# A fused attention and two-layer MLP kernel: block products of the second layer in pairs on two banks, its side work spread, the weights' sums read later

## The chip, the core and the metric

The kernel runs on one core of a Trainium2 chip. The metric is device time in microseconds (us) of one execution; the figure before is the median of three runs. Engines are named as in the profile: PE (TensorE's matmuls), PEld (TensorE's weight loads), DVE (VectorE), ACT (ScalarE), SPq (the queue of SyncE, which issues the DMAs here).

## What is computed

Eight batches of eight heads read 32 states by attention and are read by them; the result, 4352 tokens of 512 features, goes through two MLPs with squared ReLU. All of it is float32, and matmuls run as three products of split operands (a high part in fp32r and the rest), so that each product of the reference is three matmuls.

```python
def _attn_ref(x, state):                    # (8, 8, 512, 64), (8, 8, 32, 64)
    scores = scale * np.matmul(x, state.transpose(0, 1, 3, 2))
    ...softmax...;  xread = np.matmul(a, state)
    scores2 = scale * np.matmul(state, x.transpose(0, 1, 3, 2))
    ...softmax...;  sread = np.matmul(a2, x)
    return np.concatenate([xread, sread], axis=2)

x = attn_out.transpose(0, 2, 1, 3).reshape(B * S, H * D)
h = np.maximum(x @ w_in, 0.0);  x = (s * (h * h) + b) @ w_out     # first MLP: 512 -> 2048 -> 512
h = np.maximum(x @ w_in2, 0.0); out = h * h @ w_out2              # second MLP
```

## The kernel before

**The first layer** goes in steps (j, f): batch j (0 to 7, and 8 for the states' tokens) and one of 16 blocks f of 128 hidden features. A step is `mm1(j, f)` (six matmuls of 512 columns into a bank, twelve of 256 columns for j = 8), `relu2` on ACT (Relu out of the bank, Square, and Copy to the high part g), `low` on DVE (the rest of g), and `mm2` of the step two before (`LAG` = 2): twelve matmuls into four banks. I call the sixteen steps of one j a head. Work beside is hung on steps by `at_step(step, fn, rank)` and runs after the step's matmuls, in the order of rank. In heads 1 to 6 that is the attention of batch j + 1 (`att_sc` at step 3, `att_exp` and `att_norm` at 5 and 7, `att_turn` at 9 and 11, S products with two banks each at 5, 9, 13), and reading 16 pieces each of the second layer's weights `i2` and `o2` (`load_2`: a load one step, its conversion in a buffer `v` the next, and a DMA back to memory). From `i2` the sums that the block products need are made for each of eight pairs u of blocks: `sums_load` reads, `sums_add` makes four sums on DVE (tile `wt`), and seven `sums_out` each take a tile `wset`, write its high part on ACT and the rest on DVE, and send it to `w2s`. `v`, `wset` and, from step (6, 4) on, a running sum `wsum` share the pool `vp` of three buffers. Banks of `mm1`, S, scores and transposes come in turn from a cycle of four.

**The second layer** goes over six parts of up to six token tiles (the last has four) and over eight units in each, 48 in all. A unit makes two blocks of hidden features from two halves of the tokens by seven block products in the place of eight (`PRODUCTS` = 1, 6, 2, 5, 7, 3, 4). `product` is six matmuls of 384 columns (256 in the last part). Products 1, 2, 7 and 4 go to the bank A, of pool `psa`; 6, 5 and 3 to B, of `psb`; 2 adds onto 1, 3 onto 5 and 4 onto 7 in place, once what was there has been read. So one unit runs A B A B A B A, and the next begins with A. After each product ACT or DVE reads the bank, and DVE squares with max(c, 0) * c; `put_g` splits the square into the high part on ACT and the rest on DVE. The four quarters of a unit (L679, L690, L694, L697) are in the tiles `g`, which the second product `mm2_second` of the next unit reads: 36 matmuls of 512 columns (24 in the last part), of which five or six stand behind each of the seven products. Between units of a part nothing else is due; in unit 5 the next part's x is loaded, in unit 6 it gets its bias (`x_bias`) and eight differences (`x_sums`, at two products), and in unit 7 each product is followed by `x_split` of the same number: two high parts on ACT, two rests on DVE, 28 in all. For the first part all this and `o2`'s first three quarters (`load_w2`) are done in head 8, the last quarter in unit 0.

Everything is in the order of the program (`manual_schedule`): each engine takes its instructions in the order written, and waits at the head of its queue.

Of the kernel before, what the change touches and what calls it, by code (L numbers as in the profile page):

```python
# [47 lines left out]
LAG = 2  # L48
# [13 lines left out]
def attn_mlp2(ctx: ExitStack, tc: tile.TileContext, xT, xn, st, w_in1, w_out1, w_in2, w_out2, s_in, b_in, out):  # L62
# [390 lines left out]
    def mm2(j, f, g):  # L453
# [7 lines left out]
        for t in range(KD):  # L461
            sl = slice(t * P, (t + 1) * P)
            ops = [(wh[:, sl], g[:, 0]), (wh[:, sl], g[:, 1]), (wl[:, sl], g[:, 0])]
            o = acc_t[0][t][:, :n]
            for i, (l_, r_) in enumerate(ops):
                nc.tensor.matmul(out=o, lhsT=l_, rhs=r_, start=(opens and i == 0), stop=(closes and i == 2))  # L466
            if closes:
                evac(j, t, o, j < 2 and f >= CUTS[1])
# [99 lines left out]
    def x_sums(n, i, t1, t2, t3):  # L568
# [3 lines left out]
        nc.vector.tensor_tensor(out=t1, in0=a[:, th:], in1=a[:, :th], op=ALU.subtract)  # L572
        nc.vector.tensor_tensor(out=t3, in0=b[:, th:], in1=a[:, th:], op=ALU.subtract)
        nc.vector.tensor_tensor(out=t2, in0=b[:, th:], in1=t1, op=ALU.subtract)
        nc.vector.tensor_tensor(out=a[:, th:], in0=b[:, :th], in1=t2, op=ALU.subtract)
        X["t", i] = {1: a[:, :th], 2: b[:, :th], 3: b[:, th:], 4: a[:, th:], 5: t1, 6: t2, 7: t3}

    def x_split(n, m):
        v = x_view(n, m)
        for i in range(2):  # L580
            split(v[:, 0, i], v[:, 1, i], X["t", i][PRODUCTS[m]])
# [24 lines left out]
    def put_g(i, f, k, c):  # L606

        th = half(units[i][0])
        slot = xw["g", (2 * i + f) % 3]
        if k == 0:  # L610
            g2[i, f] = slot[:, : 4 * th].rearrange("p (h t) -> p h t", h=2)
        v = g2[i, f][:, :, k * th : (k + 1) * th]
        split(v[:, 0], v[:, 1], c)
# [39 lines left out]
    def second_layer(between):  # L653

        for i, (n, u) in enumerate(units):
            th = half(n)
            nn = n + 1 if n + 1 < len(parts) else None
            before = mm2_second(i - 1) if i else iter(())
            count = 6 * len(parts[units[i - 1][0]]) if i else 0
            done = 0  # L660
            c = {}
            for m, p in enumerate(PRODUCTS):
                if p == 1:
                    c["A"] = pst("A", psa)[:, :th]
                elif p == 6 or p == 5:
                    c["B"] = pst("B", psb)[:, :th]
                elif p == 7:
                    c["A"] = pst("A", psa)[:, :th]
                product(i, m, c["A" if p in (1, 2, 7, 4) else "B"], p in (1, 6, 5, 7))
                if p == 1:  # L670
                    c["m1"] = c_tile(vp, "v", th)
                    nc.scalar.copy(out=c["m1"], in_=c["A"])
                elif p == 6:
                    c["u2"] = c_tile(rp, "r", th)
                    nc.vector.tensor_tensor(out=c["u2"], in0=c["B"], in1=c["m1"], op=ALU.add)  # L675
                elif p == 2:
                    r = c_tile(at, "sc", th)
                    nc.scalar.activation(out=r, in_=c["A"], func=ACTF.Relu)
                    nc.vector.scalar_tensor_tensor(out=r, in0=c["A"], scalar=0.0, in1=r, op0=ALU.max, op1=ALU.mult)  # L679
                    c["11"] = r  # L680
                elif p == 5:
                    c["m5"] = c_tile(vp, "v", th)
                    nc.scalar.copy(out=c["m5"], in_=c["B"])
                    put_g(i, 0, 0, c["11"])
                elif p == 7:
                    c["u3"] = c_tile(vp, "v", th)
                    nc.vector.tensor_tensor(out=c["u3"], in0=c["A"], in1=c["u2"], op=ALU.add)
                elif p == 3:
                    r = c_tile(at, "sc", th)
# [293 lines left out]
```

## Time and profile before

| what | us |
|---|---|
| median of three runs (1463.84 to 1467.78) | 1465.83 |
| the profiled execution, whole | 1467.13 |
| its span, first to last instruction | 1465.3 |
| mean granted TensorE clock, share of full | 0.981 |
| PE busy | 1402.2 (96%) |
| PEld, DVE, ACT busy | 1165.5, 854.5, 641.8 |

PE is busy for almost the whole span, so the time is read from what PE does: how far apart its matmuls start, where it waits, for whom, and at which granted clock. In the timeline each row is a run of like instructions with its start, its length and, in brackets, the idle time of its engine ahead of it and what ended it. A matmul's end is modelled: a matmul of 512 columns shows as 0.39 us, and the next starts 0.23 us after it. So an idle time in brackets is some 0.16 us shorter than what the wait really took from PE.

### The profile page before, as it was taken

To read this page: it belongs to the slowest core of one execution; us is meant where nothing else is said; L and a number is where in the kernel's file an instruction comes from. 1 tells how busy PE (TensorE), PEld (TensorE's weight loads), DVE (VectorE), ACT (ScalarE), POOL (GpSimd) and SP (SyncE) were. 2 spreads that over 40 slices of the span, in tenths; PEclk is the share of its full clock that TensorE was granted. 3 is DMA by queue.
4 is the path that set the end of the run, shared out by engine and by line. 5 is a ranking of instruction groups with operands and counts; after the bars stand their busy time and mean duration, and the time that the engine had idled before them with its cause. 6 is when DMAs were issued, how large, how long until landed. Compare 5 with 4: busy or idle time off the path is not lost.

```text
span 1465.3 us, 20387 instructions
## 1 busy us (share of the span) xinstructions
PE 1402.2 (96%) x7770; PEld 1165.5 (80%) x7770; DVE 854.5 (58%) x1639; ACT 641.8 (44%) x1252; POOL 0.7 (0%) x7
## 2 busy tenths in 40 slices
PE   4999999999899999999899999999999999999998
PEld 2777777767677776889798888888888888888887
DVE  7887636466565648666534654565465447445544
ACT  4777646466566646557512322232232223222322
POOL 0000000000000000000000000000000000000000
PEclk7899999999999999999899999999999999999999
DMA  7355232535445342323635354534444453543652
GB/s 250 108 198 175 72 112 61 166 113 168 155 141 194 116 170 93 107 81 123 230 101 164 110 161 123 163 118 142 144 119 155 129 160 107 159 136 101 203 148 73
DMA packets 94017, 203.18 MB, mean 139 GB/s; under 512 B 9184, under 2 KB 26592, under 8 KB 90848
## 3 DMA queue, kind: packets, MB, share of 16 engines
q1 hardware_dynamic: 93920, 201.89, 43.2%
q8 instruction: 61, 1.00, 0.3%
q14 instruction: 36, 0.29, 0.1%
HBM read 158.86 MB, written 42.99 MB: 138 GB/s over the span
## 4 chain that ended last, share of the span: by engine, by line
PE 79%; DVE 10%; DMA 5%; ACT 4%; issue 1%; SPq 1%; ACTq 0%; DVEq 0%
PE o L631 22%; PE acc L466 20%; PE A L594 12%; PE h L436 11%; PE B L594 9%; PE S L255 1%; PE sr L401 1%; DMA w2s<-wset 1%; DMA xT<-xT 1%; DVE sc L604 1%; DVE sc L690 1%; DMA o2r<-w_out 1%; DMA i<-v 1%; DMA i2r<-w_in 1%; DMA ws<-i 1%
## 5 line engine op out<-in xcount | busy, mean ns | idle before, releaser
L466 PE MATMUL acc<-g,o1h 128*128 128x512 f32 (+1 forms) x1152 | 345.0, 382 | 1.9 <-ACT g L445 1.3
L466 PEld LDWEIGHTS acc<-g,o1h 128*128 128x128 f32 x1152 | 213.4, 190 | 46.8 <-issue 2.2
L436 PE MATMUL h<-aT,S 128*128 128x512 f32 x768 | 207.2, 406 | 15.0 <-ACT r L443 9.8
L466 PE MATMUL acc<-g,o1l 128*128 128x512 f32 (+1 forms) x576 | 219.0, 380 | 0.4 <-DVE o1l L189 0.4
L436 PEld LDWEIGHTS h<-aT,S 128*128 128x128 f32 x768 | 143.1, 192 | 66.9 <-issue 12.5
L449 DVE TENSOR_TENSOR g<-r,g 128x512 fp32r<-128x512 f32 (+1 forms) x144 | 95.1, 661 | 155.0 <-ACT g L445 152.3
L466 PEld LDWEIGHTS acc<-g,o1l 128*128 128x128 f32 x576 | 109.2, 190 | 21.6 <-DVE o1l L189 0.9
L631 PE MATMUL o<-o2h,xw('g', 0)_6560 128*128 128x512 f32 x364 | 124.5, 395 | 0.0
L631 PE MATMUL o<-o2h,xw('g', 1)_6561 128*128 128x512 f32 x364 | 123.7, 393 | 0.0
L631 PE MATMUL o<-o2h,xw('g', 2)_6562 128*128 128x512 f32 x360 | 122.6, 393 | 0.0
L443 ACT ACTIVATE r<-h 128x512 f32<-128x512 f32 (+1 forms) x144 | 81.8, 568 | 84.3 <-PE h L436 82.0
L594 PE MATMUL A<-xw 128*128 128x384 f32 (+1 forms) x576 | 112.8, 330 | 4.4 <-DVE t L697 3.7
L594 PEld LDWEIGHTS A<-xw 128*128 128x128 f32 x576 | 98.9, 188 | 16.7 <-DVE t L697 9.4
L444 ACT ACTIVATE r<-r 128x512 f32<-128x512 f32 (+1 forms) x144 | 87.6, 608 | 4.6
L445 ACT ACTIVATE g<-r 128x512 fp32r<-128x512 f32 (+1 forms) x144 | 87.6, 608 | 4.6
L594 PE MATMUL B<-xw 128*128 128x384 f32 (+1 forms) x432 | 84.1, 329 | 0.2 <-DVE r L675 0.2
L594 PEld LDWEIGHTS B<-xw 128*128 128x128 f32 x432 | 75.7, 188 | 6.2 <-DVE r L675 0.6
L631 PEld LDWEIGHTS o<-o2h,xw('g', 0)_6560 128*128 128x128 f32 x364 | 68.1, 189 | 9.9
L631 PEld LDWEIGHTS o<-o2h,xw('g', 1)_6561 128*128 128x128 f32 x364 | 67.6, 188 | 10.0
L594 PE MATMUL A<-xw,xw('odd', 0)_6433 128*128 128x384 f32 (+1 forms) x288 | 58.2, 337 | 17.3 <-DVE t L697 17.3
L631 PEld LDWEIGHTS o<-o2h,xw('g', 2)_6562 128*128 128x128 f32 x360 | 66.9, 188 | 9.8
L631 PE MATMUL o<-o2l,xw('g', 0)_6560 128*128 128x512 f32 x182 | 72.1, 396 | 0.0
(147 smaller groups left out, 2013.7 us busy)
## 6 DMA issues: line engine op xcount, KB each, us to landing
xw<-w2s SPq DMA_DIRECT2D x168, 256.0 KB, 2.7
xw('odd', 0)_6433<-w2s SPq DMA_DIRECT2D x24, 1024.0 KB, 5.0
xw('odd', 1)_6434<-w2s SPq DMA_DIRECT2D x24, 768.0 KB, 4.3
w2s<-wset SPq DMA_DIRECT2D x56, 256.0 KB, 2.3
i1r<-w_in SPq DMA_DIRECT2D x16, 512.0 KB, 4.9
xT<-xT SPq DMA_DIRECT2D x16, 512.0 KB, 5.7
xn<-xn SPq DMA_DIRECT2D x8, 1024.0 KB, 8.1
o1r<-w_out SPq DMA_DIRECT2D x16, 512.0 KB, 4.3
```

The costliest lines, as they stand in the source:

```text
L255: nc.tensor.matmul(out=outs[r][k * NS : (k + 1) * NS], lhsT=state[rows, r, k, :], rhs=moving(rows, k), start=True, stop=True, skip_group_c ...
L401: nc.tensor.matmul(out=srp[r * D : (r + 1) * D, k * NS : (k + 1) * NS], lhsT=n[:, i, h * D : (h + 1) * D], rhs=a2Ts[r][:, i, k * NS : (k + ...
L436: nc.tensor.matmul(out=hp, lhsT=l_, rhs=r_, start=(i == 0), stop=(i == len(ops) - 1))
L443: nc.scalar.activation(out=r, in_=hp, func=ACTF.Relu)
L444: nc.scalar.activation(out=r, in_=r, func=ACTF.Square)
L445: nc.scalar.activation(out=g[:, 0], in_=r, func=ACTF.Copy)
L449: nc.vector.tensor_tensor(out=g[:, 1], in0=r, in1=g[:, 0].bitcast(F32), op=ALU.subtract)
L466: nc.tensor.matmul(out=o, lhsT=l_, rhs=r_, start=(opens and i == 0), stop=(closes and i == 2))
L594: nc.tensor.matmul(out=o, lhsT=w[:, a, k, :], rhs=x[:, b, k, :], start=(start and k + a + b == 0), stop=(k + a == 2), skip_group_check=True,)
L604: nc.vector.scalar_tensor_tensor(out=c, in0=c, scalar=0.0, in1=c, op0=ALU.max, op1=ALU.mult)
L631: nc.tensor.matmul(out=acc2[t], lhsT=l_, rhs=r_, start=(fa == 0 and e == 0), stop=(fa == NF - 1 and e == 2))
L690: nc.vector.tensor_tensor(out=r, in0=c["B"], in1=c["u2"], op=ALU.add)
```

## The change

It makes no product less or more. (1) In the second layer the banks alternate with every product, across units too; two products stand in a row (a pair), and behind each pair ten or eleven matmuls of the second product. (2) The last two steps' `mm2` of the first layer (24 matmuls, the generator `rest`) are taken out of its end and stand as shares between the products of unit 0. (3) The drain is written anew: out of bank 1 + 2 DVE no longer multiplies; Relu, and Square on ACT in two instructions, for three quarters of four; the split's two halves stand a product or more behind each other. (4) `x_load` moves from unit 5 to unit 3, `x_bias` from 6 to 4, `x_sums` is dealt out singly over units 5 and 6, and `x_split`'s 28 instructions over eleven products, of which the last four are the next part's first. (5) `o2`'s second to fourth quarter are read and split in units 0 to 2. (6) The sums of pair u are loaded, added and sent at head 3 + u // 2, from step 1 or 9: added four steps after the load, and sent one per step at seven steps, where it was two per step at four.

```diff
+        flow = [(rest, 2 * KD * 3)]
+        def drain(i, m, out):
+            p, th = PRODUCTS[m], half(units[i][0])
+            ...
+            if p == 1:
+                c["m1"] = c_tile(vp, "v", th)
+                act(c["m1"], out, ACTF.Copy)
+            elif p == 6:
+                add(c["u2"], out, c["m1"])
+            elif p == 2:
+                act(r, out, ACTF.Relu)
+                after[i, m + 1] = [lambda: act(r, r, ACTF.Square), lambda: g_hi(i, 0, 0, r)]
+                after[i, m + 2] = [lambda: g_lo(i, 0, 0, r)]
+            ...
+            elif p == 3:
+                add(r, out, c["u2"])
+                add(q, c["u3"], c["m5"])
+                act(r, r, ACTF.Relu)
+                act(r, r, ACTF.Square)
+                g_hi(i, 0, 1, r)
+                after[i, m + 1] = [lambda: g_lo(i, 0, 1, r), lambda: square(q)]
+                after[i + 1, 0] = [lambda: g_hi(i, 1, 1, q)]
+                after[i + 1, 1] = [lambda: g_lo(i, 1, 1, q)]
+            elif p == 4:
+                add(r, out, c["u2"])
+                after[i + 1, 0] = [
+                    lambda: act(r, r, ACTF.Relu), lambda: act(r, r, ACTF.Square), lambda: g_hi(i, 1, 0, r)
+                ] + after[i + 1, 0]
...
+            job(3, 6, lambda: x_load(n))
+            for k in range(KD):
+                job(4, 3 + k, lambda k=k: x_bias(k))
+            job(5, 0, begin)
+            for e in range(8):
+                job(5, 1 + 3 * e // 2, lambda e=e: sums[e]())
+            for e in range(count):
+                m, i = e // 2, e % 2
+                job(7, 11 * e // count, lambda m=m, i=i: x_hi(n, m, i))
+                job(7, 11 * e // count + 1, lambda m=m, i=i: x_lo(n, m, i))
...
+                step = i * len(PRODUCTS) + m
+                pool = (psa, psb)[step % 2]
+                if p in (1, 6, 5, 7):
+                    c[p] = pst(f"m{p}", pool)[:, :th]
+                out = c[{2: 1, 3: 5, 4: 7}.get(p, p)]
+                product(i, m, out, p in (1, 6, 5, 7))
+                drain(i, m, out)
+                if step % 2:
+                    while len(flow) > 1:
+                        for _ in flow.pop(0)[0]:
+                            pass
+                        done = 0
+                    upto = flow[0][1] * (m + 1) // len(PRODUCTS)
...
-    for u, (j, f) in enumerate(((2, 13), (3, 5), (3, 12), (4, 3), (4, 10), (5, 1), (5, 9), (6, 1))):
+    for u in range(NF // 2):
+        at0 = step(3 + u // 2, 8 if u % 2 else 0)
         box = {}
-        at_step(step(j, f), lambda u=u, box=box: box.update(raw=sums_load(u)), 7)
-        at_step(step(j, f) + 2, lambda u=u, box=box: box.update(src=sums_add(u, box["raw"])), 8)
+        at_step(at0 + 1, lambda u=u, box=box: box.update(raw=sums_load(u)), 7)
+        at_step(at0 + 5, lambda u=u, box=box: box.update(src=sums_add(u, box["raw"])), 8)
         for m in range(len(PRODUCTS)):
-            at_step(step(j, f) + 3 + m // 2, lambda u=u, m=m, box=box: sums_out(u, m, box["src"]), 8)
+            at_step(at0 + 6 + m, lambda u=u, m=m, box=box: sums_out(u, m, box["src"]), 8)
...
-            if q < 3:
-                at_step(s8 + 11 + 2 * q + h, load, 9)
-                at_step(s8 + 13 + 2 * q + h, cut, 9)
+            if q < 1:
+                at_step(s8 + 11 + h, load, 9)
+                at_step(s8 + 13 + h, cut, 9)
             else:
-                between.setdefault((0, h), []).append(load)
-                between.setdefault((0, 4 + h), []).append(cut)
+                between.setdefault((q - 1, 3 * h), []).append(load)
+                between.setdefault((q - 1, 3 * h + 3), []).append(cut)
```

How the order of three queues moves: on PE, the end of unit 0 and the beginning of unit 1, before (xw is the tile with a product's weights and x, the odd unit's weights are in xw('odd', 0)):

```order
L594 MATMUL A<-xw_6129 128x384 x6
L594 MATMUL B<-xw_6285 128x384 x6
L594 MATMUL A<-xw_6286 128x384 x6
L594 MATMUL A<-xw_5994,xw('odd', 0)_6433 128x384 x6
L631 MATMUL o_6697<-o2h_6468,xw('g', 0)_6560 128x512
L631 MATMUL o_6697<-o2l_6469,xw('g', 0)_6560 128x512
L631 MATMUL o_6697<-o2h_6468,xw('g', 0)_6560 128x512
L631 MATMUL o_6698<-o2h_6468,xw('g', 0)_6560 128x512
L631 MATMUL o_6698<-o2l_6469,xw('g', 0)_6560 128x512
L594 MATMUL B<-xw_5995,xw('odd', 0)_6433 128x384 x6
```

The same place after (the acc rows are `rest`, of the first layer):

```order
L610 MATMUL m_6603<-xw_6129 128x384 x6
L610 MATMUL m_6578<-xw_6285 128x384 x6
L466 MATMUL acc_6028<-g,o1h_1267 128x256
L466 MATMUL acc_6028<-g,o1l_1268 128x256
L466 MATMUL acc_6029<-g,o1h_1267 128x256 x2
L466 MATMUL acc_6029<-g,o1l_1268 128x256
L466 MATMUL acc_6030<-g,o1h_1267 128x256 x2
L610 MATMUL m_6603<-xw_6286 128x384 x6
L610 MATMUL m_6654<-xw_5994,xw('odd', 0)_6433 128x384 x6
```

The product that opens unit 1 (the one that reads `xw('odd', 0)`) wrote the same bank as the one ahead of it, and now writes the other; the seven matmuls of the first layer stand between the pairs.

On DVE, the end of unit 7 of the first part (`xw5` and `xw6` are `x_split`'s rests for the next part, L697 is the read that frees bank A for the next unit's first product), before:

```order
L694 TENSOR_TENSOR t1_7512<-v_7490,v_7470 128x384
L111 TENSOR_TENSOR xw5_6285<-x12_7200,xw5_6285 128x384
L111 TENSOR_TENSOR xw5_6285<-x13_7203,xw5_6285 128x384
L697 TENSOR_TENSOR t1_7530<-A_7483,r_7433 128x384
L604 SCALAR_TENSOR_TENSOR t1_7530<-t1_7530 128x384
L111 TENSOR_TENSOR xw('g', 0)_6560<-t1_7530,xw('g', 0)_6560 128x384
L604 SCALAR_TENSOR_TENSOR t1_7512<-t1_7512 128x384
L111 TENSOR_TENSOR xw('g', 0)_6560<-t1_7512,xw('g', 0)_6560 128x384
L111 TENSOR_TENSOR xw6_6286<-x10_7194,xw6_6286 128x384
L111 TENSOR_TENSOR xw6_6286<-x11_7197,xw6_6286 128x384
```

After (L689 with m7 is that read now):

```order
L689 TENSOR_TENSOR t1_7516<-v_7492,v_7478 128x384
L590 TENSOR_TENSOR xw3_6128<-t0_7190,xw3_6128 128x384
L689 TENSOR_TENSOR t1_7530<-m7_7485,r_7443 128x384
L637 TENSOR_TENSOR xw('g', 2)_6540<-sc_7514,xw('g', 2)_6540 128x384
L620 SCALAR_TENSOR_TENSOR t1_7516<-t1_7516 128x384
L590 TENSOR_TENSOR xw3_6128<-t0_7190,xw3_6128 128x384
L590 TENSOR_TENSOR xw4_6129<-t2_7192,xw4_6129 128x384
L689 TENSOR_TENSOR r_7572<-m6_7564,v_7555 128x384
```

One rest stands ahead of the read where there were two, and `xw5` and `xw6` have gone on into the next part's first unit.

On ACT, from step 7's conversion to step 9's Relu in head 4 (h48 is the bank of step (4, 8)), before:

```order
L126 ACTIVATE v_3614<-i2r30_3561 128x512
L110 ACTIVATE wset_3621<-ws3_3447 128x256
L110 ACTIVATE wset_3625<-wt3_3531 128x256
L443 ACTIVATE r_3636<-h48_3629 128x512
L444 ACTIVATE r_3636<-r_3636 128x512
L445 ACTIVATE g_3637<-r_3636 128x512
L110 ACTIVATE wset_3654<-wt3_3531 128x256
L110 ACTIVATE wset_3658<-wt3_3531 128x256
L443 ACTIVATE r_3669<-h49_3662 128x512
```

After:

```order
L126 ACTIVATE v_3575<-i2r30_3526 128x512
L110 ACTIVATE wset_3582<-wt2_3496 128x256
L443 ACTIVATE r_3593<-h48_3586 128x512
L444 ACTIVATE r_3593<-r_3593 128x512
L445 ACTIVATE g_3594<-r_3593 128x512
L110 ACTIVATE wset_3611<-ws2_3319 128x256
L443 ACTIVATE r_3622<-h49_3615 128x512
```

A step carries one `wset` where it carried two; heads 3, 5 and 6, which had one pattern each, have this one too.

## Rows read from the trace of the kernel before

**Rows 1.** Windows (columns in the first line): head 2; 3-6; 4; units 0-1; 2-39.

```profile
core 0: us, PE busy (x) PEld busy (x) DVE busy (x) ACT busy (x) POOL busy (x), PEclk, DMA share, GB/s
194.74:269.64 74.90, 74.90 (x442) 57.45 (x440) 41.23 (x74) 43.50 (x75) 0.00 (x0) 1.00 0.36 104
269.64:594.18 324.54, 309.14 (x1762) 233.88 (x1760) 200.09 (x388) 197.13 (x364) 0.00 (x0) 0.97 0.43 146
350.76:433.83 83.07, 76.80 (x442) 58.37 (x441) 49.08 (x98) 50.13 (x96) 0.00 (x0) 0.96 0.47 157
713.22:747.41 34.19, 26.88 (x122) 23.73 (x121) 17.73 (x30) 9.99 (x17) 0.00 (x0) 0.85 0.41 133
747.41:1363.03 615.62, 602.29 (x2965) 536.65 (x2965) 329.57 (x635) 160.92 (x346) 0.00 (x0) 1.00 0.45 136
```

**Rows 2.** Window of one undisturbed unit, from its first product to the next's.

```profile
794.67:810.42 15.75, 15.75 (x79) 14.12 (x79) 6.99 (x14) 3.34 (x7) 0.00 (x0) 1.00 0.62 186
```

**Rows 3.** Who waited for whom: total us, times, longest.

```profile
PE A L594 <- DVE t L697: 21.0, 21, 6.3
ACT wset L110 <- DMA i<-v: 20.1, 4, 8.4
```

**Rows 4.** Timeline of PE: first products of units 7, 8, 43.

```profile
828.30 1.31 PE L594 MATMUL A<-xw,xw('odd', 0)_6433 128*128 128x384 f32 x6 [1.96 <-DVE t L697]
844.97 1.31 PE L594 MATMUL A<-xw 128*128 128x384 f32 x6 [0.66 <-DVE t L697]
...
1398.98 0.98 PE L594 MATMUL A<-xw,xw('odd', 0)_6433 128*128 128x256 f32 x6 [0.21 <-DVE t L697]
```

**Rows 5.** Timeline of the end of unit 0, all engines.

```profile
722.12 1.06 ACT L110 ACTIVATE o2h<-o2f 128x1024 fp32r<-128x1024 f32 x1 [2.10 <-DMA o2f<-o]
723.21 1.23 DVE L111 TENSOR_TENSOR o2l<-o2f,o2h 128x1024 fp32r<-128x1024 f32 x1 [2.13 <-ACT o2h L110]
...
728.17 0.55 DVE L697 TENSOR_TENSOR t<-A,r 128x384 f32<-128x384 f32 x1
...
728.78 2.29 PE L594 MATMUL A<-xw,xw('odd', 0)_6433 128*128 128x384 f32 x6 [6.34 <-DVE t L697]
```

**Rows 6.** Timeline of PE: two products in a row; one between shares; the last share.

```profile
718.91 1.20 PE L594 MATMUL A<-xw 128*128 128x384 f32 x6
719.95 1.21 PE L594 MATMUL B<-xw 128*128 128x384 f32 x6
...
781.11 1.23 PE L594 MATMUL B<-xw 128*128 128x384 f32 x6
782.18 0.63 PE L631 MATMUL o<-o2h,xw('g', 0)_6560 128*128 128x512 f32 x2
...
783.33 1.23 PE L594 MATMUL A<-xw 128*128 128x384 f32 x6
...
1454.22 0.62 PE L631 MATMUL o<-o2h,xw('g', 1)_6561 128*128 128x512 f32 x2
...
1454.90 0.62 PE L631 MATMUL o<-o2h,xw('g', 1)_6561 128*128 128x512 f32 x2
```

**Rows 7.** Groups of instructions by shape: busy us, mean ns | idle before.

```profile
L594 PEld LDWEIGHTS A<-xw 128*128 128x128 f32 x576 | 98.9, 188 | 16.7 <-DVE t L697 9.4 <-ACT v L672 1.5 <-DVE v L687 0.3
L444 ACT ACTIVATE r<-r 128x512 f32<-128x512 f32 x128 | 80.9, 632 | 4.1
L110 ACT ACTIVATE xw('g', 0)_6560<-sc 128x384 fp32r<-128x384 f32 x28 | 14.7, 526 | 57.8 <-DVE sc L604 57.8
L110 ACT ACTIVATE wset<-wt 128x256 fp32r<-128x256 f32 x32 | 13.1, 412 | 20.2 <-DMA i<-v 10.9 <-DMA o<-v 6.3 <-DMA w2s<-wset 1.6
```

**Rows 8.** Timeline: conversions that waited in head 4; `mm1` of step 10, heads 4 and 5.

```profile
402.55 0.91 ACT L110 ACTIVATE wset<-wt 128x256 fp32r<-128x256 f32 x2 [2.43 <-DMA i<-v]
...
404.00 2.92 PE L436 MATMUL h<-aT,S 128*128 128x512 f32 x6 [4.50 <-ACT r L443]
...
482.27 2.86 PE L436 MATMUL h<-aT,S 128*128 128x512 f32 x6 [1.16 <-ACT r L443]
```

More of the change, by code (lines that the diff above doesn't have):

```diff
@@ L655, in second_layer @@
         for i, (n, u) in enumerate(units):
             th = half(n)
[L657 to L661, printed above, removed]
-            for m, p in enumerate(PRODUCTS):
[L663 to L689, printed above, removed]
-                    nc.vector.tensor_tensor(out=r, in0=c["B"], in1=c["u2"], op=ALU.add)
-                    square(r)
-                    put_g(i, 0, 1, r)
-                    c["22"] = c_tile(at, "t1", th)
-                    nc.vector.tensor_tensor(out=c["22"], in0=c["u3"], in1=c["m5"], op=ALU.add)
-                elif p == 4:
-                    r = c_tile(at, "t1", th)
-                    nc.vector.tensor_tensor(out=r, in0=c["A"], in1=c["u2"], op=ALU.add)
-                    square(r)
-                    put_g(i, 1, 0, r)
-                    square(c["22"])
-                    put_g(i, 1, 1, c["22"])
-                upto = count * (m + 1) // len(PRODUCTS)
-                for _ in itertools.islice(before, upto - done):
-                    pass
-                done = upto
-                for fn in between.pop((i, m), []):
-                    fn()
-                if nn is not None:
-                    if (u, m) == (5, 2):
-                        x_load(nn)
-                    elif u == 6 and m < KD:
-                        x_bias(m)
-                    elif u == 6 and m in (4, 5):
-                        if m == 4:
-                            x_temps(nn)
-                        x_sums(nn, m - 4, *(X["s", t][:, m - 4] for t in range(3)))
-                    elif u == 7:
-                        x_split(nn, m)
@@ L720, in second_layer @@
+        for m in range(2):
+            for fn in after.pop((len(units), m), []):
+                fn()
+        for g, _ in flow:
+            for _ in g:
                 pass
@@ L722, in second_layer @@
             pass
-        assert not between, sorted(between)
+        assert not jobs and not after, (sorted(jobs), sorted(after))
     side = {}
@@ L940, in attn_mlp2 @@
         assert not side, sorted(side)
-        second_layer(between)
+        last = range(len(order) - LAG, len(order))
+        second_layer(between, itertools.chain(*(mm2(*order[i], gs.pop(i)) for i in last)))
 _OUTS = [((NT, DM), "float32")]
```

99 lines of the change are left out of this document (78 added, 21 removed).

## Prediction

> **What bounds the kernel now.** I read the windows by stage first: where PE is busy all the time only fewer or closer matmuls help, and elsewhere the idle time can be priced. Head 2 is full: 74.90 us, all busy, at the full clock [rows 1]. Heads 3 to 6 do the same matmuls and take 324.54, so 24.9 us more than four times 74.90. Of that 15.4 is idle (324.54 - 309.14) and 9.5 is the same work at a lower granted clock, 0.97 in the mean (309.14 - 299.60). Units 0 and 1 take 34.19 us with 7.3 idle and a clock of 0.85. Units 2 to 39 take 615.62; an undisturbed unit takes 15.75 [rows 2], 38 of them 598.5, so 17.1 are lost at a full clock. Then the waits: in the second layer PE waited 21.0 us, 21 times, for one thing, L697 on DVE, which frees bank A for the next unit's first product [rows 3]. The timeline says where: units 7 and 8, on either side of a part's end, wait 1.96 and 0.66, and each unit of the last part from the third on 0.21 [rows 4]; unit 1 waited 6.34 [rows 5]. A wait costs some 0.16 more than its idle, since a matmul's row outlasts the next one's start by that.
>
> **The entry to the second layer.** Before, seven products stand in a row with nothing between, and DVE reaches L697 late: it sits behind a rest of `o2`, which waited 2.13 for ACT, which waited 2.10 for a read from memory [rows 5]. Then comes a stretch at a lower clock (0.85 over this window [rows 1]). Now 24 short matmuls, which PE did anyway, fill the gaps, and unit 1 opens on the other bank. Without waits unit 0 has seven products of 1.04 (719.95 - 718.91 [rows 6]), 7.3 us, and unit 1 some 15.6: 22.9 against 34.19, 11.3 less. New here are two pieces of `o2` that are split in unit 0 itself, three products after their read is issued: the last such read in front of the wait shows that one can come late by 2.10. DVE then does a rest of 1.23 ahead of reading product 7's bank, which product 4 wants two and a half microseconds after. I put 1.3 us of waits there, between 0 and 4. Gain 10.0. This falls away only if PE waits as long for something else; next late would be that read.
>
> **The parts' ends and the last part.** The loss in units 2 to 39 is 17.1 us [rows 1, 2], and in the last part six waits of 0.21 with 0.16 each, 2.3 [rows 4]. They have one cause: the last product and the next unit's first share bank A, with five matmuls (1.15 us) between, while in unit 7 DVE has 28 - 14 = 14 rests and in unit 6 eight differences in front of the read. With alternating banks, between the end of a product and the next on its bank lie one other product and ten matmuls, 1.04 + 2.3 = 3.3 us, everywhere, and ahead of a read there stands at most one or two rests of about 0.55. Going through unit 7 and the next part's first unit by hand with the durations of these rows, I find each bank read a microsecond or more ahead of the product that wants it. So 19.4 goes. For waits that I don't see I leave 3.0 (0 to 10, half of what goes): a late rest of x, or ACT.
>
> **Pairs.** A product between shares takes 1.07 (782.18 - 781.11), one behind another 1.04 [rows 6]: a change from 512 to 384 columns costs 27 ns. Five matmuls of the share take 1.15 (783.33 - 782.18), while in the long last share three take 0.68, 227 ns each, 20 ns less over five. There are half as many changes, 3.5 less per unit. The 27 ns are certain, 0.095 us a unit or 3.7 over units 1 to 39; of the 20 I take a half, since no share of ten is in the trace: 1.5 (0 to 2.7). Sum 5.2.
>
> What the pairs ask of the weight loads is the place where a rule weighs in. The rows show loads of 188 ns each [rows 7] under matmuls that start 173 apart for six in a row. The Trainium skill ("TensorE: Matmul & The Clock Gate", section "LDWEIGHTS (loading the stationary operand)") gives columns / 1.2 ns; an estimate from it is 107 ns for 128 columns, well under 173. By that rule a load always fits under the matmul ahead of it, rival C has no ground and the sum stays; by the row's 188 a longer run of short matmuls could fall behind its loads. The trace differs from the page in the duration, and no row says what twelve in a row do between long matmuls, which is rival C.
>
> The same page (section "A second HAM failure mode: psum-queue depth-cycling") says that PE's small waits between groups on cycling banks make the clock swing. Here the granted clock stood at 1.00 through all waits of units 2 to 39 [rows 1], so nothing is added for a clock that comes back there; by the rule the 17.1 would hold some of that and the gain would be the same 17.1, differently named.
>
> **ACT and DVE in the units.** ACT gains Square for three quarters and a Relu for two, five instructions of some 0.53 (estimate, by the copy of 384 columns and the square of 512 [rows 7]), DVE loses four of about 0.55 a unit (as L697 [rows 5]). ACT goes from 3.34 to about 6 of 15.75 [rows 2]. Neither is near its limit: nothing for it, while the 3.3 us cover it.
>
> **The heads of the first layer.** What is queued where: on ACT the conversions `wset` stand ahead of the next step's Relu, and from the first exponential (step 5) to the Relu of step 9 ACT never catches up, so each conversion of 0.41 [rows 7] there moves that Relu, whose bank step 10 wants. In head 2 nothing stands there and PE doesn't wait. In head 4 conversions waited for a buffer, the write of `v` (2.43), and step 10 came 4.50 late; in head 5 one or two sufficed for 1.16 more [rows 8]. After, every head has three conversions in that place (steps 6, 7, 8), 1.2 us: less than head 4 had, more than head 5. On top I put 0.6 in heads 4 to 6, where a conversion at step 3 waits for the write of `v` from step 1, behind the next batch's loads and now the sums' too on SP's queue; and in head 6, where `wsum` holds one of three buffers, 2.4 for the conversion of step 8, which needs the buffer that `v` took in step 7 (the nearest row is the 2.43). Idle: 1.2 + 1.8 + 1.8 + 4.2 = 9.0; with the clock at the same ratio, 9.5 / 15.4, 5.6 more. So 14.6 of 24.9 stay, and 10 go. The bounds are far apart: all of it (24.9), or a loss of 8 (rival A).
>
> **The sum.** 10.0 + 19.4 - 3.0 + 5.2 + 10 = 41.6 us off the profiled execution's 1467.13, which lies 1.3 over the median. Against the median 1465.83: 1424.
>
> **Rivals.** A: the sums' new places cost. Every head gets conversions where the attention is densest, and if each then is like head 4 (83.07 [rows 1], 8.17 over head 2), heads 3 to 6 lose 32.7, 7.8 more than now: 1465.8 - 31.6 + 7.8 = 1442. For it: DVE's share in head 6, where the running sums stand too; against: head 4 had two conversions per step, and waits for buffers that one per step seldom meets.
> B: the parts' ends go on waiting. x's rests now sit in the next part's first unit, in front of its reads, and `x_sums` between the reads of units 5 and 6; if half of the 19.4 stays, 1424 + 10 = 1434. Against: two or three microseconds of room.
> C: weight loads bind in longer runs. If twelve matmuls of 384 columns go at 188 ns, a pair takes 2.26 in place of 2.13, 0.12 more at 3.5 pairs of 39 units, 16.7 us, and the 3.7 are not won: 1445. Against: two products in a row in unit 0, 1.04 for the first, six at 173 [rows 6].
> D, slower: ACT becomes the link. It does Relu, Square, Copy of a quarter in a row, 1.6 us, between bank reads. If it runs 3.3 us behind, each unit's first product waits for its predecessor's read, 47 times; from 41.6 / 47 = 0.9 us per unit the kernel is slower, at 1.1 it is 1476. Against: 6 us of work in 15.6; for: nothing but the strict order.
> E: the heads' waits all go, 1424 - 15 = 1409.
>
> **Chances.** Forecast 0.66 (own range 1414 to 1434), B 0.12, A 0.09, C 0.06, E 0.04, D 0.03. The range reaches over B and A, and to 1411 on the other side, for the pairs' and the entry's upper bounds. A measurement of this kernel tells 0.3% (4.4 us) from no change. All cases but D lie further below: faster 0.95; of the rest slower 0.03, the same 0.02.
>
> **What would show it.** Right: the product that opens a unit has no idle in front of it; units of 15.6 us on either side of a part's end; the window of units 0 and 1 near 24 with a clock of 1.00; two products in 2.10; step 10 of heads 3 to 5 waiting 1 to 2 us. Wrong: PE waiting for ACT in L594's place, now L610 (D); weight loads with idle but no releaser and pairs over 2.2 (C); idle at parts' ends (B); heads of over 82 us (A).

## The result and the profile after

The changed kernel takes 1422.49 us (median of four runs, 1421.1 to 1423.36) beside 1466.71 for the kernel before: ratio 0.9701, 95% interval 0.9684 to 0.9718. That is 44.2 us less. The forecast was 1424: 41.6 less than the median of 1465.83 that stood before, which one more run has moved to 1466.71. The profiled spans are 1465.3 and 1421.6, 43.7 apart, and the windows by stage say where these went. The windows of the changed kernel: heads 2, 3, 4, 5 and 6, units 0 and 1, units 2 to 39, the rest, and two units (8 and 9) of the second layer.

```profile
core 0: us, PE busy (x) PEld busy (x) DVE busy (x) ACT busy (x) POOL busy (x), PEclk, DMA share, GB/s
195.92:270.92 75.00, 75.00 (x441) 57.45 (x440) 41.22 (x74) 43.46 (x75) 0.00 (x0) 1.00 0.34 97
270.92:346.70 75.78, 75.05 (x441) 57.45 (x440) 45.42 (x88) 47.55 (x86) 0.00 (x0) 1.00 0.39 131
346.70:423.03 76.33, 74.78 (x442) 57.32 (x440) 47.39 (x94) 48.93 (x91) 0.00 (x0) 1.00 0.47 157
423.03:500.94 77.91, 75.47 (x441) 57.38 (x440) 47.43 (x94) 48.91 (x91) 0.00 (x0) 1.00 0.45 154
500.94:584.17 83.23, 78.30 (x442) 59.51 (x440) 56.59 (x109) 49.38 (x91) 0.00 (x0) 0.96 0.41 143
700.33:727.29 26.96, 26.35 (x146) 24.28 (x145) 13.65 (x24) 13.36 (x26) 0.00 (x0) 1.00 0.66 215
727.29:1322.88 595.59, 595.59 (x2965) 536.68 (x2964) 260.23 (x519) 257.75 (x536) 0.00 (x0) 1.00 0.46 143
1322.88:1421.60 98.72, 92.72 (x565) 82.83 (x563) 37.06 (x94) 42.62 (x110) 0.00 (x0) 0.99 0.45 144
821.34:852.69 31.35, 31.35 (x158) 28.25 (x157) 15.33 (x30) 15.24 (x32) 0.00 (x0) 1.00 0.52 169
```

Read beside [rows 1]: heads 3 to 6 fall from 324.54 to 313.25 (11.3 less). Units 0 and 1 go from 34.19 to 26.96, although the first layer's last 24 matmuls now stand in them; heads 7 and 8, which lost these, go from 119.04 to 116.16, so the entry gains 7.23 + 2.88 = 10.1. Units 2 to 39 go from 615.62 to 595.59 (20.0 less), with PE busy all the time. From unit 40 to the end 102.27 becomes 98.72 (3.6 less). The start, up to head 2, is 1.2 later and head 2 itself 0.1 longer. Sum 43.7. The first layer differs from trace to trace: in the traces of this study head 2 starts between 193.97 and 196.23, and heads 3 to 6 with the new table of sums take 309.9 to 313.3 in the eight traces that share all else there. The 313.25 of this trace is the longest of them.

The second layer has one wait left, 0.48 us for a read by DVE, in unit 0, and two products in a row take 2.11 (760.75 - 758.64), the ten matmuls behind them 2.30 (763.05 - 760.75), as the timeline of PE shows:

```profile
709.60 1.33 PE L610 MATMUL m<-xw 128*128 128x384 f32 x6 [0.48 <-DVE v L689]
...
758.64 2.27 PE L610 MATMUL m<-xw 128*128 128x384 f32 x12
760.75 0.39 PE L655 MATMUL o<-o2h,xw('g', 0)_6538 128*128 128x512 f32 x1
...
763.05 2.27 PE L610 MATMUL m<-xw 128*128 128x384 f32 x12
```

In the heads step 10 still waits, 0.73 in head 3, 1.46 in heads 4 and 5, and in head 6 3.96, behind a conversion on ACT that waited 2.39 for a buffer (timeline of PE and ACT; the rows answer to [rows 8]):

```profile
394.67 1.65 PE L436 MATMUL h<-aT,S 128*128 128x512 f32 x6 [1.46 <-ACT r L443]
...
552.05 0.42 ACT L110 ACTIVATE wset<-ws 128x256 fp32r<-128x256 f32 x1 [2.39 <-DMA o<-v]
...
553.00 2.93 PE L436 MATMUL h<-aT,S 128*128 128x512 f32 x6 [3.96 <-ACT r L443]
```

Of the waits in these four heads a lower clock follows that one alone: heads 3 to 5 stand at 1.00 in the windows above, and the 4 us from 553.00 on at 0.50:

```profile
553.00:557.00 4.00, 4.00 (x9) 3.15 (x10) 2.51 (x4) 2.37 (x5) 0.00 (x0) 0.50 0.81 240
```

### The profile page after: what moved, and what is told of

Its sections match the earlier page's. It is cut to its first block, busy times and chain, and to the rows that moved or that the text cites. A ratio compares the mean times of both kernels' runs of the same rounds, so it can differ in the third digit from the quotient of the medians.

```text
span 1421.6 us, 20393 instructions
## 1 busy us (share of the span) xinstructions
PE 1383.8 (97%) x7770; PEld 1162.1 (82%) x7770; DVE 767.6 (54%) x1495; ACT 755.8 (53%) x1492; POOL 0.7 (0%) x7
## 4 chain that ended last, share of the span: by engine, by line
PE 86%; DVE 5%; ACT 4%; DMA 3%; issue 1%; SPq 0%; ACTq 0%; DVEq 0%
PE o L655 26%; PE m L610 23%; PE acc L466 21%; PE h L436 12%; PE S L255 1%; PE sr L401 1%; ACT r L444 1%; ACT r L443 1%; DMA o<-v 1%; DMA o2r<-w_out 1%; DMA i<-v 1%; PE S L283 1%; ACT g L445 1%; PE sc L255 1%; DVE g L449 1%
## 5 line engine op out<-in xcount | busy, mean ns | idle before, releaser
L610 PE MATMUL m<-xw 128*128 128x384 f32 (+1 forms) x1008 | 183.2, 328 | 0.5 <-DVE v L689 0.5
L610 PEld LDWEIGHTS m<-xw 128*128 128x128 f32 x1008 | 171.6, 188 | 8.1 <-DVE v L689 0.7
L623 ACT ACTIVATE sc<-sc 128x384 f32<-128x384 f32 (+1 forms) x144 | 72.7, 505 | 157.9 <-DVE sc L689 156.4
L623 ACT ACTIVATE v<-m 128x384 f32<-128x384 f32 (+1 forms) x96 | 45.5, 474 | 156.0 <-PE m L610 155.4
L655 PE MATMUL o<-o2h,xw('g', 0)_6538 128*128 128x512 f32 x364 | 121.2, 392 | 0.0
L655 PE MATMUL o<-o2h,xw('g', 1)_6539 128*128 128x512 f32 x364 | 121.1, 392 | 0.0
L655 PE MATMUL o<-o2h,xw('g', 2)_6540 128*128 128x512 f32 x360 | 119.8, 392 | 0.0
L689 DVE TENSOR_TENSOR v<-m,r 128x384 f32<-128x384 f32 (+1 forms) x48 | 25.7, 535 | 168.9 <-PE m L610 168.9
L610 PE MATMUL m<-xw,xw('odd', 0)_6433 128*128 128x384 f32 (+1 forms) x576 | 107.3, 328 | 0.0
L610 PEld LDWEIGHTS m<-xw,xw('odd', 0)_6433 128*128 128x128 f32 x576 | 98.4, 188 | 3.8
L689 DVE TENSOR_TENSOR r<-m,v 128x384 f32<-128x384 f32 (+1 forms) x48 | 25.7, 535 | 105.3 <-PE m L610 87.5
L610 PE MATMUL m<-xw,xw('odd', 1)_6434 128*128 128x384 f32 (+1 forms) x432 | 79.5, 327 | 0.1
```

Source lines behind the costliest of these rows:

```text
L610: nc.tensor.matmul(out=o, lhsT=w[:, a, k, :], rhs=x[:, b, k, :], start=(start and k + a + b == 0), stop=(k + a == 2), skip_group_check=True,)
L623: nc.scalar.activation(out=c, in_=src, func=func)
L655: nc.tensor.matmul(out=acc2[t], lhsT=l_, rhs=r_, start=(fa == 0 and e == 0), stop=(fa == NF - 1 and e == 2))
L689: add = lambda o, x, y: nc.vector.tensor_tensor(out=o, in0=x, in1=y, op=ALU.add)
```

## The experiments

Times in the expectations are in us. Where I speak of units 2 to 39 or of units 0 and 1, it is the time from the first matmul of the first to the first matmul after the last, as in the windows.

**The sums' places, undone.** The changed kernel with the old table.

```diff
-    for u in range(NF // 2):
-        at0 = step(3 + u // 2, 8 if u % 2 else 0)
+    for u, (j, f) in enumerate(((2, 13), (3, 5), (3, 12), (4, 3), (4, 10), (5, 1), (5, 9), (6, 1))):
```

> The changed kernel with the sums of the eight pairs at their old steps, all else as changed. If the sums' places alone made heads 3 to 6 shorter (324.5 us before, 313.3 after), they take about 324.5 again, with step 10 of head 4 waiting 4.5 us for ACT, and the time is 1422.5 + 11.3 = 1434 us. Rival: part of the gain came with something else in those heads, for instance a different drift of the buffers; then the heads stay near 313 and the time near 1422.

It took 1432.84 (ratio to before 0.9775, 0.9759 to 0.9791), 10.4 more than the changed kernel; heads 3 to 6 take 323.32. In head 4 ACT and PE do what they did before, within a hundredth (timeline):

```profile
401.72 0.90 ACT L110 ACTIVATE wset<-wt 128x256 fp32r<-128x256 f32 x2 [2.44 <-DMA i<-v]
...
403.16 2.93 PE L436 MATMUL h<-aT,S 128*128 128x512 f32 x6 [4.49 <-ACT r L443]
```

So the heads' gain comes with the sums' places and is independent of the second layer: three traces with the old table (before, this one and that of alternating banks alone) have 324.54, 323.32 and 323.18, and none with the new one is over 313.25.

**Even pairs later.** Conversions out of the stretch between step 5 and the Relu of step 9.

```diff
-            at_step(at0 + 6 + m, ...
+            at_step(at0 + (6 + m if u % 2 else 10 + m // 2), ...
```

> The changed kernel with the seven conversions of every even pair moved from steps 6 to 12 to steps 10 to 13 of their head, two at a step; the odd pairs stay. If every wait left in heads 3 to 6 comes from the conversions between the first exponential (step 5) and the Relu of step 9, step 10 no longer waits there, each head takes about 75.0 us, the four 300 in place of 313.3, and the time is about 1409 us. Rival: the waits come from the attention's own chain beside the other work of these heads (conversions of the weights, running sums on DVE), then they stay and the time is 1422 us. Between: only the 0.4 us conversions go and head 6 keeps its wait for a buffer, 1416 us.

1416.59 (0.9661, 0.9647 to 0.9676), the middle outcome. Heads 3, 4 and 5 take 75.34, 74.63 and 75.72: there the theory holds, but for a wait of 1.05 that step 10 of head 5 keeps. Head 6 keeps 81.53, with its wait in another place (timeline of ACT and PE):

```profile
558.97 0.42 ACT L110 ACTIVATE wset<-wt 128x256 fp32r<-128x256 f32 x1 [5.62 <-DMA o<-v]
...
561.25 0.49 PE L466 MATMUL acc<-g,o1h 128*128 128x512 f32 x1 [2.43 <-ACT g L445]
```

The conversion waits for the write of `v` to leave its buffer, and the `g` of step 11, queued behind it on ACT, comes late for `mm2`.

**The running sum in another pool.** No engine's instruction moves; only the buffer is another.

```diff
-            sums["w"] = vp.tile([P, 512], F32, tag="v", name="wsum")
+            sums["w"] = op.tile([P, 512], F32, tag="o", name="wsum")
```

> The changed kernel with the running sum wsum in a buffer of another pool, so that v and wset have all three of vp to themselves in head 6; every engine's instructions stay the same and in the same order. If head 6 (83.2 us, against 77.9 of head 5) is long because the conversion of step 8 waits 2.39 us for the buffer that v holds, that wait goes, step 10 waits about 1.5 us as in heads 4 and 5, head 6 takes about 78 us, and the time is about 1417 us. Rival: head 6 is long because DVE has the running sums to add (56.6 us of work there against 47.4), then it stays at 83 and the time at 1422 us.

1416.6 (0.9662, 0.9648 to 0.9677). Head 6 takes 78.31 with a full clock, and DVE is as busy as it was (55.74 beside 56.59), so its load was not the cause. The window of head 6:

```profile
499.63:577.94 78.31, 75.82 (x442) 57.50 (x440) 55.74 (x109) 49.01 (x91) 0.00 (x0) 1.00 0.43 150
```

In the timeline the conversion at 548.67 waits for nothing, and step 10 waits as in heads 4 and 5:

```profile
548.67 0.40 ACT L110 ACTIVATE wset<-ws 128x256 fp32r<-128x256 f32 x1
...
549.61 1.66 PE L436 MATMUL h<-aT,S 128*128 128x512 f32 x6 [1.46 <-ACT r L443]
```

**Both together.**

> The changed kernel with both edits that helped apart: the even pairs' conversions at steps 10 to 13 and the running sum in another pool. With the even pairs late, what is left in head 6 are waits at steps 11 to 13 behind a conversion that waits 5.62 us for a buffer that v holds; with three buffers for v and wset these go too, heads 3 to 6 take some 75.5 each, 302 us, and the time is about 1411 us. Rival: v and wset, two at a step, still want more buffers than three, head 6 keeps half of its waits, 1414 us or more.

1412.65 (0.9629, 0.9609 to 0.965; 1410.56 to 1414.03), the best kernel of this study, 10 us below the changed one. The four heads take 75.20, 74.78, 75.48 and 77.16, 302.6 in place of the expected 302. The windows of heads 3 to 7:

```profile
269.42:344.62 75.20, 75.20 (x441) 57.46 (x440) 45.43 (x88) 47.60 (x86) 0.00 (x0) 1.00 0.40 132
344.62:419.40 74.78, 74.74 (x442) 57.34 (x440) 47.47 (x94) 49.23 (x91) 0.00 (x0) 1.00 0.49 161
419.40:494.88 75.48, 74.70 (x441) 57.35 (x440) 47.35 (x94) 48.90 (x91) 0.00 (x0) 1.00 0.47 159
494.88:572.04 77.16, 75.80 (x442) 57.46 (x440) 54.14 (x106) 48.57 (x90) 0.00 (x0) 1.00 0.43 150
572.04:640.79 68.75, 67.79 (x313) 54.97 (x312) 47.49 (x83) 41.39 (x72) 0.00 (x0) 1.00 0.38 125
```

The last row is head 7, 1.3 longer than in the changed kernel (67.49), with 0.96 of it idle behind a drain on ACT into a tile of the pool that now also holds `wsum`. With `wsum` there alone head 7 took 67.52, so what brings that wait about stays open.

**No pairs.** A share behind every product, banks alternating.

```diff
-                if step % 2:
+                if True:
```

> The changed kernel with a share of the second product behind every product in place of every second, banks still alternating with every product. If alternating banks alone take the waits away, PE never waits in units 2 to 39 and a unit takes 15.75 us in place of 15.68: 3 us more there, about 4 over the layer, 1426 us. Rival: the drain as now written needs the ten or eleven matmuls behind a pair, then each unit waits 0.3 to 1 us for DVE or ACT, 12 to 40 us more, 1437 to 1465 us.

1424.98 (0.972, 0.9703 to 0.9736), 2.5 more than with pairs, within what such runs leave open; the trace is sharper. A unit takes 15.75, and units 2 to 39 598.62 beside 595.59, without one wait. The pairs are worth 3.0 there and are not what keeps PE from waiting. The window of a unit:

```profile
819.77:835.52 15.75, 15.75 (x80) 14.19 (x78) 9.59 (x20) 8.99 (x19) 0.00 (x0) 1.00 0.60 193
```

**Old banks, with pairs.**

```diff
-                pool = (psa, psb)[step % 2]
+                pool = psa if p in (1, 2, 7, 4) else psb
```

> The changed kernel with the banks given out as before (products 1, 2, 7 and 4 on the one, 6, 5 and 3 on the other), pairs and all else as changed. At every second border of two units a pair then lies on one bank, and its second product has to wait until DVE has read the first: 24 times about 0.9 us (a read of 0.55 and the way to it and back), 21 us, 1444 us. Rival: the spread side work alone took the waits away, then 1422 us.

1442.35 (0.9817, 0.9798 to 0.9837), 19.9 more. A product that follows its predecessor on the same bank starts 0.81 us late (0.65 idle and the 0.16 that a row hides), 24 times, and itself takes 1.17 (774.67 - 773.50) where a product in a row takes 1.04. The wait list (who waited for whom: total us, times, longest):

```profile
PE m L610 <- DVE t L689: 15.4, 24, 0.9
```

One such product, and the matmul behind it, in the timeline of PE:

```profile
773.50 1.33 PE L610 MATMUL m<-xw,xw('odd', 0)_6433 128*128 128x384 f32 x6 [0.65 <-DVE t L689]
774.67 0.39 PE L655 MATMUL o<-o2h,xw('g', 1)_6539 128*128 128x512 f32 x1
```

And the window of units 2 to 39:

```profile
726.10:1339.22 613.12, 600.76 (x2965) 535.68 (x2964) 260.23 (x519) 256.76 (x535) 0.00 (x0) 1.00 0.44 138
```

Pairs need alternating banks. The granted clock stays at 1.00 with such a wait in every second unit. The Trainium skill ("TensorE: Matmul & The Clock Gate", section "A second HAM failure mode: psum-queue depth-cycling") lets small idles between groups on cycling banks swing the clock; for waits of 0.65 us every 32 us this trace does not show it.

**Old banks, no pairs.** Both edits at once.

> The changed kernel with the banks given out as before and a share behind every product; what stays of the change in the second layer is the drain, the spread work on x and o2, and the shares of unit 0. If the same bank at the border of two units was the cause of the waits by itself, those of the parts' ends (3.74 a part's end and 0.37 a unit in the last part before) come back in most part: 1426 + 15 = about 1441 us. Rival: DVE's queue of rests ahead of the read was the cause, and since that is spread now the 1.15 us of five matmuls are enough, but for the last part, whose shares are shorter: 1426 to 1430 us.

1424.77 (0.9701, 0.9684 to 0.9718), the same as with alternating banks and no pairs (1424.98). Units 2 to 39 take 598.63, and PE waits twice in the whole layer, both in unit 0 (wait list):

```profile
PE m L610 <- DVE v L689: 0.9, 1, 0.9
...
PE m L610 <- DVE t L689: 0.5, 1, 0.5
```

The theory fell here: the shared bank was not the cause by itself. With the work on x spread and the new drain, five matmuls between two products on one bank are enough, even at the parts' ends.

**x packed.** The next part's bias, differences and split at their old places, banks and pairs as changed.

```diff
-            job(3, 6, lambda: x_load(n))
+            job(5, 2, lambda: x_load(n))
...
-                job(4, 3 + k, lambda k=k: x_bias(k))
+                job(6, k, lambda k=k: x_bias(k))
...
-                job(5, 1 + 3 * e // 2, lambda e=e: sums[e]())
+                job(6, 4 + e // 4, lambda e=e: sums[e]())
...
-                job(7, 11 * e // count, lambda m=m, i=i: x_hi(n, m, i))
-                job(7, 11 * e // count + 1, lambda m=m, i=i: x_lo(n, m, i))
+                job(7, m, lambda m=m, i=i: x_hi(n, m, i))
+                job(7, m, lambda m=m, i=i: x_lo(n, m, i))
```

> The changed kernel with the work on the next part's x at its old places: bias and differences in unit 6, two high parts and two rests after every product of unit 7. If alternating banks leave 3.3 us for each read everywhere, two rests of 0.55 ahead of it don't matter and units 6 to 8 of a part stay at 14.3 and 17.0 us: 1422 us. Rival: they do matter, and each part's end waits 0.5 to 2 us: 5 ends, 1425 to 1432 us.

1423.15 (0.9692, 0.9672 to 0.9711): no difference from the changed kernel. Units 2 to 39 take 596.43, 0.8 more: four first units of a part take 14.52 in place of 14.31. With alternating banks, pairs and the new drain, spreading x is worth no more than that.

**The new drain alone.** Old banks, no pairs, x packed.

> The changed kernel with banks as before, a share behind every product, and the work on the next part's x at its old places: of the change in the second layer the new drain (two squares on ACT, four instructions of DVE fewer), o2's places and the shares of unit 0 are left. With x spread this kernel had no wait in units 2 to 39 and took 1424.8 us. If spreading x was what cleared the reads at the parts' ends, units 7, 8 and their like wait again, some 3.7 us for each of five ends, 1440 to 1443 us. Rival: fewer instructions on DVE were enough, then 1425 us.

1432.15 (0.9768, 0.9745 to 0.9791), between the two expectations. Units 2 to 39 take 607.66, 9.2 over 38 times 15.75, where the kernel before lost 17.1. The wait list:

```profile
PE m L610 <- DVE t L689: 7.2, 10, 0.9
```

The first products of two units at a part's end in the timeline of PE, as in [rows 4]:

```profile
803.55 1.13 PE L610 MATMUL m<-xw,xw('odd', 0)_6433 128*128 128x384 f32 x5 [0.68 <-DVE t L689]
...
820.49 1.32 PE L610 MATMUL m<-xw 128*128 128x384 f32 x6 [0.93 <-DVE t L689]
```

So the new drain removes about half, and the waits of the last part's later units (a unit 10.55 where it was 11.03); spreading x removes the rest. Which part of the drain does it, the squares taken off DVE or the new order of its instructions, no run tells apart.

**Alternating banks alone**, in the kernel before.

```diff
-                    c["A"] = pst("A", psa)[:, :th]
+                    c["A"] = pst("A", (psa, psb)[i % 2])[:, :th]
-                    c["B"] = pst("B", psb)[:, :th]
+                    c["B"] = pst("B", (psb, psa)[i % 2])[:, :th]
```

> The kernel before with one edit: the two banks change places from unit to unit, so that a unit's first product never has the bank of the last one. Drain, work on x, o2, sums and shares stay as before. If alternating banks alone suffice, unit 1's opening wait (6.3 us), the waits at the parts' ends (17.1 us over units 2 to 39) and those of the last part (2.3) go: 1467 - 26, about 1441 us. Rival: DVE's queue of rests and squares then holds up another read (a product in unit 7 or 8 waits for DVE in another place), and no more than half goes: 1450 to 1457 us.

1449.08 (0.9876, 0.9851 to 0.9901): 19 less than before where the one expectation said 26 and the other at most half. Units 2 to 39 take 605.08, so 6.6 of the 17.1 stay, and PE waits for another engine, ACT (wait list):

```profile
PE A L594 <- ACT v L672: 6.0, 11, 0.7
```

One of these waits in the timeline of ACT and PE:

```profile
825.12 0.52 ACT L110 ACTIVATE xw('g', 1)_6561<-t 128x384 fp32r<-128x384 f32 x1 [1.18 <-DVE t L604]
825.55 0.46 ACT L672 COPY v<-A 128x384 f32<-128x384 f32 x1
826.06 1.31 PE L594 MATMUL A<-xw,xw('odd', 0)_6433 128*128 128x384 f32 x6 [0.74 <-ACT v L672]
```

The copy that frees product 1's bank stands on ACT behind a high part, and that waits for DVE's square, which is behind DVE's rests. The queue on DVE reaches PE by way of ACT. In units 0 and 1 the other bank alone is worth 4.1 (34.19 before, 30.09 here), with `o2` at its old places:

```profile
711.86:741.95 30.09, 26.00 (x122) 22.55 (x121) 17.62 (x30) 10.00 (x17) 0.00 (x0) 0.94 0.47 151
```

**The entry.** First the 24 matmuls alone back in front of unit 0 (the first hunk), then also `o2` at its old places (all of it).

```diff
+        for i in last:
+            for _ in mm2(*order[i], gs.pop(i)):
+                pass
-        second_layer(between, itertools.chain(*(mm2(*order[i], gs.pop(i)) for i in last)))
+        second_layer(between, iter(()))
...
-            if q < 1:
-                at_step(s8 + 11 + h, load, 9)
-                at_step(s8 + 13 + h, cut, 9)
+            if q < 3:
+                at_step(s8 + 11 + 2 * q + h, load, 9)
+                at_step(s8 + 13 + 2 * q + h, cut, 9)
...
-                between.setdefault((q - 1, 3 * h), []).append(load)
-                between.setdefault((q - 1, 3 * h + 3), []).append(cut)
+                between.setdefault((0, h), []).append(load)
+                between.setdefault((0, 4 + h), []).append(cut)
```

> The changed kernel with the last 24 matmuls of the first layer back in front of unit 0, whose seven products then stand in a row on alternating banks. A bank is then wanted again 1.04 us after its product ends, and a read takes 0.47 to 0.55 with one rest or another ahead: five times 0.3 to 1 us, and maybe a lower clock behind it: 1424 to 1428 us. Rival: the entry's gain came from the pieces of o2 that went to units 1 and 2, then 1422 us.

1423.66 (0.9694, 0.9674 to 0.9713), not to be told from the changed kernel. By the traces heads 7 and 8 take 119.05 and units 0 and 1 26.10, together 145.2 where the changed kernel has 116.16 + 26.96 = 143.1: 2.0 us. PE waits once, 2.76, in units 0 and 1 (timeline, cut off after five matmuls), and their window stands at a clock of 1.00:

```profile
708.54 1.14 PE L610 MATMUL m<-xw 128*128 128x384 f32 x5 [2.76 <-DVE v L689]
...
699.37:725.47 26.10, 23.34 (x123) 21.33 (x121) 12.99 (x23) 14.02 (x25) 0.00 (x0) 1.00 0.64 224
```

> The changed kernel with the entry as before: the last 24 matmuls of the first layer in front of unit 0, and o2's second and third quarter in head 8, the fourth in unit 0. Beside the kernel with the 24 matmuls alone put back (units 0 and 1 26.1 us, 1423.7 us in all), it tells what o2's places do. If late pieces of o2 ahead of DVE's reads cost, units 0 and 1 take 2 to 4 us more, 1426 to 1428 us. Rival: alternating banks alone made the entry short, then 1424 us.

1428.82 (0.9739, 0.9719 to 0.976). Units 0 and 1 take 32.63, 6.5 more than with the 24 matmuls alone put back, and the timeline shows the chain of [rows 5] again, under alternating banks:

```profile
711.31 1.06 ACT L110 ACTIVATE o2h<-o2f 128x1024 fp32r<-128x1024 f32 x1 [4.14 <-DMA o2f<-o]
712.40 1.23 DVE L111 TENSOR_TENSOR o2l<-o2f,o2h 128x1024 fp32r<-128x1024 f32 x1 [4.62 <-ACT o2h L110]
713.54 0.55 DVE L689 TENSOR_TENSOR sc<-m,r 128x384 f32<-128x384 f32 x1
...
714.14 2.29 PE L610 MATMUL m<-xw,xw('odd', 0)_6433 128*128 128x384 f32 x6 [5.34 <-DVE sc L689]
```

A read of `o2` lands late, ACT waits for it, DVE waits for ACT, and PE for the bank behind DVE. An earlier piece, which lands 1.31 late, costs PE another 1.29 by way of ACT's queue.

## Why the prediction came out

**The heads** (10 forecast, 11.3 measured): right, with its reason, though the size is surer than its closeness tells: other traces of the same heads are up to 3.4 shorter. Idle time was put at 1.2, 1.8, 1.8 and 4.2 in heads 3 to 6; it is 0.73, 1.55, 2.44 and 4.93 (span less PE's busy time). Head 6's extra wait is the one named, `wset` behind `v` with `wsum` in the pool, 2.39 where 2.4 was put, and the run with `wsum` elsewhere took it away. The 5.6 for the clock was mis-sized: the ratio was applied to every wait, and heads 3 to 5 ran at 1.00; only head 6's 3.96 was followed by a lower clock. PE's busy time over four times 74.90 came to 4.0 (303.60 - 299.60), 3.4 of it in head 6. Rival A, conversions as dear as in head 4, is refuted by the windows of heads 3 to 5. Head 6, at 83.23, shows the sign named for A (over 82 us), but it falls to 78.31 with the same conversions and `wsum` elsewhere. Rival E, that all the heads' waits go, took two more edits to come near: 302.6, where four times 74.90 is 299.6.

**The entry** (10.0 forecast, 10.1 measured): the size is right. The sign "a window near 24" left out the 24 matmuls, 2.88 us, that the change puts into that window. The reason was given as the other bank and the filled gaps; taken back from the changed kernel one after the other, the gaps filled are 2.0, `o2`'s late pieces 6.5, and 1.6 is left for bank and drain together. Put alone into the kernel before, the other bank was worth 4.1; so the shares hang on the order in which the edits are made, and what is shown is that `o2`'s old places cost 6.5 even on alternating banks. The rest of `o2` that was feared in unit 0 cost 0.48 where 1.3 was put, and not by a late read: ACT's conversion there waits for nothing.

**The parts' ends and the last part** (19.4 - 3.0 forecast): the outcome is right, all of it went and the 3.0 for unseen waits was not needed. The step that gives the cause was wrong: "They have one cause", the shared bank. Units 2 to 39 lose 17.1 in the kernel before, 6.6 with alternating banks alone, 9.2 with the new drain alone, nothing that shows (0.1) with drain and spread x on the old banks, 0.8 beside the changed kernel with drain, alternation and pairs but x packed. DVE's queue ahead of the read and the short way between two products on a bank were both needed for the whole loss; alternating banks alone take 10.5 of it, the new drain alone 7.9, and the new drain with either spread x or alternating banks (these with pairs) leaves no more than a microsecond. The old drain with spread x was not run. That the whole loss went in spite of the wrong cause is partly luck: the change eased the queue as well as the banks. Working through unit 7 by hand showed that the changed kernel has room, not which edit makes it. Rival B did not come about, since PE never waits in units 2 to 39. With alternating banks alone some waits did stay, but under the old drain and by way of ACT's copy, which B does not name.

**Pairs** (5.2 forecast, about 3 measured): a unit takes 15.75 without and, in the mean of two, 15.675 with pairs, 0.075 less, 2.9 over units 1 to 39. The term was mis-sized in both halves. The second: a matmul of the share was to come down toward 227 ns in longer shares, by the last share's rows; in shares of ten it takes 230 (2.30 / 10), as in shares of five (1.15 / 5). The first, called certain: a pair does gain the 27 ns, 2.11 for two where two apart took 2.14, but the product that opens a unit had nothing to gain. In the kernel before it takes 1.04 (795.71 - 794.67) with a share on either side, the next one 1.07 (797.93 - 796.86), in the timeline of PE:

```profile
794.67 1.20 PE L594 MATMUL A<-xw,xw('odd', 0)_6433 128*128 128x384 f32 x6
795.71 0.39 PE L631 MATMUL o<-o2h,xw('g', 2)_6562 128*128 128x512 f32 x1
...
796.86 1.23 PE L594 MATMUL B<-xw,xw('odd', 0)_6433 128*128 128x384 f32 x6
797.93 0.63 PE L631 MATMUL o<-o2h,xw('g', 2)_6562 128*128 128x512 f32 x2
```

So six products of a unit paid the 27 ns before, and 3.5 pay them now: 27 ns x 2.5 x 39 is 2.6, near the 2.9. Rival C is refuted by these same 2.11: twelve in a row run at the pace of six.

**ACT** (nothing forecast): units 8 and 9, with x's high parts in them, keep ACT busy for 7.6 us each (units 2 to 39 6.8 in the mean, 257.75 / 38, where about 6 was put), and PE never waits for it. The squares take 523 ns for 384 columns, where 0.53 was estimated (groups by shape: busy us, mean ns | idle before):

```profile
L623 ACT ACTIVATE sc<-sc 128x384 f32<-128x384 f32 x120 | 62.8, 523 | 138.0 <-DVE sc L689 136.8
```

Rival D did not come about.

Put together, forecast and measured: heads 10 and 11.3, entry 10.0 and 10.1, parts' ends, last part and pairs 21.6 and 23.6, the start's 1.3 the other way: 41.6 and 43.7. The unneeded 3.0 and the 2.3 too many for the pairs nearly cancel; of the 2.0 left over, 1.3 is the last part, which gained 3.6 where 2.3 was put (six times 0.37 is 2.2): a unit there took 11.03 with its wait and takes 10.55 without, 0.48, in part because the product behind a wait is itself longer (rows of 1.31 in [rows 4], of 1.20 to 1.23 in [rows 6]). That two misses cancel, and that the heads came out within 1.3, is luck; that each stage gains about what was put is not.

## What to carry to other kernels

A wait that one row shows between two engines may need two conditions, here a short way back to the same bank and a queue ahead of the read; work out what each edit does alone before calling one of them the cause, since the cheaper may do. Side work goes where the engine that carries the pace has slack in its own queue, and its buffers count as much as its time: a long-lived tile in a small pool made one head 3 to 5 us longer (81.4 to 83.2 in the traces with the new table, 78.3 with the tile elsewhere) without an instruction being added to it. A piece of work that waits for memory should not stand ahead of the read that frees a bank.

## What the runs showed of the hardware

Where matmuls of 384 and 512 columns take turns, the share's matmuls stay at 230 ns in shares of five and of ten, against 227 in the last, long share [rows 6]; I had taken that excess for something that longer shares would halve. The product's six matmuls behind a share take 1.07 where the next six take 1.04, but the product that opens a unit takes 1.04 behind its share too. So the 27 ns are not the change of size alone, and what makes them stays open.

The length of a wait alone does not tell whether the granted clock falls. PE waits of 0.73 to 1.46 us in heads 3 to 5 of the changed kernel, and 24 waits of 0.64 in the mean in the run with old banks and pairs, left it at 1.00 (2.4 GHz). The 3.96 of head 6 was followed by 0.50 (1.2 GHz) over the next 4 us, and the 5.34 of the run with the old entry by a product of 2.29 us, where one takes 1.2 to 1.3. But in head 5 of the kernel before a wait of 1.16 was followed by six matmuls in 2.86 [rows 8], where six take 1.65 at the full clock (the granted clock is 0.57 from 482 to 486 there), and with the 24 matmuls back in front of unit 0 a wait of 2.76 left the clock at 1.00. What else decides it stays open.
